# Attention into a token mixer on one core: the hand-ordered steps behind batch 0's first products in another order, with two more filling products

## The chip, the cores and the metric

The kernel runs on one core of one Trainium2 chip. The metric is the device time of one execution in microseconds (us). Three runs of the kernel before gave 104.08, 104.41 and 104.64; the median, 104.41, is what the change is held against.

## The reference

Eight batches, eight heads, 576 tokens, head size 64, float32 in and out. Each batch goes through an attention in two stages over 32 packed queries `p`, and the result goes, heads side by side (576 x 512), into a mixer whose mixing matrix is made from the tokens themselves.

```
p_packed = softmax(p k^T / 8) v            # per head: 32 x 64
x        = softmax(q p_packed^T / 8) p_packed   # per head: 576 x 64, then 576 x 512
wq, wk   = x @ w_q, x @ w_k                # 576 x 64 each
W_tok    = (wq wk^T) / 8                   # 576 x 576, never formed by the kernel
mixed    = W_tok @ x
out      = relu(mixed) @ w_out             # 576 x 512
```

## The kernel before, in words

There is no loop in the program. A string, `ORDER` (lines 13 to 57), lists some 520 steps, and lines 603 to 624 issue them one after the other. Each step runs on one engine, and each engine executes its own steps in the order in which the string has them: a step that has to wait holds back whatever stands behind it on that engine. Semaphores for the data that steps exchange are set by the framework. A token reads `STEP.batch.part@engine=PSUM banks`: `@A` is ScalarE (ACT), `@V` VectorE (DVE), `@P` GpSimd (POOL); matmul steps have no engine and are TensorE's (PE). The eight PSUM banks are named by hand after the `=`.

The steps of one batch b, in the order of their data:

- `LD.kb`, `LD.vb`, `LD.qb` load k, v and q with a cast to bf16. GpSimd issues them, each `LD.v` as two transfers, every other one as one. They share GpSimd's instruction stream with its arithmetic. There are four buffers of each (`NL = 4`).
- `KT` (DVE) transposes k; `S1` (PE) forms the scores of the packed queries; `X1` (ACT) takes the exponential; `TE` (DVE) transposes it; `PV` (PE) multiplies with v and with a column of ones; `RC`, `PP`, `PT` (DVE) divide and transpose. That gives p_packed.
- `QK` (PE) multiplies p_packed with w_k and w_q; `QKE` copies it out of PSUM, and `QD` (POOL) copies a half of it once more.
- `QV` (DVE) transposes q; `S2` (PE) forms the scores of the 576 queries in parts (0 and 1: 256 tokens each, 2: the last 64, 3: 512 tokens); `X2` (ACT) takes the exponential into float32; `RS` and `RR` (DVE) sum and take reciprocals; `AM` multiplies, on POOL or DVE, into bf16; `AT` (PE) transposes and `AE` copies that out.
- `WKQ` (PE) forms wk and wq from it, `WE` copies; `GM`, `GE`, `Y`, `YE` build the small matrix of the mixer; `MX` and `MR` (PE) form the mixed tokens, `RL` and `RLR` apply the relu; `OT.b.0` to `OT.b.3` (PE) multiply 128 tokens each with w_out, `OT.b.4` what remains of two batches (odd b alone); `OE` and `OEF` copy to SBUF, `ST` and `STF` store to memory, nearly all issued by SyncE (SP), a few by POOL.
- `WARM.n=bank` is work without a result: TensorE multiplies zeros, 128n columns in float32, 512 columns at a time unless a second number says otherwise.

Output tiles `o` have six buffers (`NO = 6`, line 8), so batch 6 writes where batch 0 was, and batch 7 where batch 1 was: `OE.6` needs `ST.0` finished. `HOLD.v7` makes SP, whose stores stand behind it, wait until v of batch 7 has landed.

The order of work between `WKQ.0` and `S1.3`, which the prediction walks through, stands on lines 20 to 29. Of GpSimd's steps it holds these, in the kernel before:

```
AM.0.1 LD.q2 LD.O LD.k3 LD.v3 QD.1 AM.1.2 AM.1.0 AM.1.1 LD.k4 QD.2 LD.q3 LD.v4 LD.q4 AM.2.3 AM.2.2 LD.k5
```

Of the kernel before, what the change touches and what calls it, by code (L numbers as in the profile page):

```python
# [28 lines left out]
RL.1.1@A S1.3=2,3,0,1 X1.3.0@A AM.2.2@P OT.1.4=4 TE.3.0@V LD.k5 AT.2.2=5 X1.3.1@A TE.3.1@V AT.2.3=2 AE.2.3@V
LD.v5 MX.1.0=6,7 AE.2.2@V PV.3.0=0,1 PV.3.1 OEF.1.4@A WKQ.2.0=2,3 WKQ.2.1 RC.3@V PP.3.1@V RL.1.0@A WKQ.2.2  # L30
WE.2.2@A OT.1.2=4,5 OT.1.3 PP.3.0@V PT.3@V QK.3=6 OE.1.1@A LD.q5 KT.4.2@V S1.4=0,1,2,3 GM.2=7 OT.1.0=4,5
X1.4.1@A LD.k6 GE.2@A QKE.3@V X1.4.0@A QV.3.2@V TE.4.1@V Y.2=2,3 YE.2@A S2.3.2=6,7 X2.3.2@A S2.3.3=0,1
X2.3.3@A MX.2.0=2,3 TE.4.0@V RL.2.0@A MR.2=6,7 RLR.2@V OT.1.1 MX.2.1=6,7 RL.2.1@A OE.1.0@A PV.4.0=0,1 QD.3@P
PV.4.1 RS.3.4@V RR.3.4@V LD.v6 AM.3.3@P AM.3.2@P RC.4@V OT.2.0=2,3 OT.2.1 LD.q6 OE.2.0@A PP.4.0@V PP.4.1@V
PT.4@V QK.4=6 AT.3.3=7 QV.4.2@V AT.3.2=0 AE.3.2@A LD.k7 S2.4.2=4,5 AE.3.3@V X2.4.2@A S2.4.3=2,3 X2.4.3@A
KT.5.2@V WKQ.3.0=0,1 WKQ.3.1 WKQ.3.2 RS.4.4@V RR.4.4@V QKE.4@A WE.3.2@A S1.5=4,5,2,3 X1.5.1@A LD.v7 TE.5.1@V
OT.2.2=6,7 AM.4.3@P QD.4@P AM.4.2@P GM.3=0 X1.5.0@A TE.5.0@V GE.3@A OT.2.3 Y.3=2,3 YE.3@V PV.5.0=4,5 PV.5.1
HOLD.v7 MR.3=0,1 RC.5@V PP.5.1@V OE.2.1@A MX.3.0=2,3 PP.5.0@V PT.5@V MX.3.1=6,7 RLR.3@A RL.3.0@A OT.3.4=0
RL.3.1@A AT.4.2=1 AE.4.2@A OEF.3.4@A QV.5.2@V AT.4.3=5 AE.4.3@V ST.1.4@P QK.5=4 QKE.5@V QD.5@P S2.5.2=2,3
X2.5.2@A KT.6.2@V S2.5.3=6,7 X2.5.3@A HA.5@P WKQ.4.0=0,1 WKQ.4.2 LD.q7 WKQ.4.1 WE.4.2@A OT.3.0=2,3  # L40
S1.6=4,5,6,7 X1.6.0@A GM.4=0 GE.4@V TE.6.0@V LD.r7 OT.3.1 X1.6.1@A TE.6.1@V Y.4=0,1 OE.3.0@A RS.5.4@V RR.5.4@V
PV.6.0=4,5 YE.4@A PV.6.1 MX.4.0=6,7 RC.6@V RL.4.0@A PP.6.0@V AM.5.3@P PP.6.1@V PT.6@V MX.4.1=2,3 AM.5.2@P
OT.3.2=0,1 OT.3.3 RL.4.1@A QK.6=4 QKE.6@A QV.6.2@V ST.2.1 S2.6.2=6,7 X2.6.2@A S2.6.3=2,3 ST.3.4 MR.4=4,5
# [5 lines left out]
OEF.5.4@A S2.7.1=6,7 ST.5.4 GM.6=3 GE.6@V X2.7.1@A RS.7.1@V RR.7.1@V S2.7.2=0,1 X2.7.2@A S2.7.0=4,5 QK.7=2
X2.7.0@A RS.7.0@V RR.7.0@V Y.6=6,7 YE.6@A OT.5.2=0,1 MX.6.1=4,5 QKE.7@A MX.6.0=6,7 AM.7.1@P RS.7.2@V RR.7.2@V  # L50
MR.6=2,3 OT.5.3 RLR.6@V RL.6.0@V RL.6.1@A OE.5.1@A ST.4.1 AM.7.0@P OT.5.0=2,3 AM.7.2@P AT.7.0=4 AE.7.0@A
AT.7.1=5 AE.7.1@V AT.7.2=6 AE.7.2@V OT.6.2=0,1 OEF.6.2@A QD.7@P WKQ.7.0=4,5 WKQ.7.2 WKQ.7.1 WE.7.0@A WE.7.1@A
STF.6.2 OT.6.0=6,7 OT.6.1 GM.7=0 OE.6.0@V OT.5.1 OE.5.0@V ST.5.1 GE.7@A Y.7=4,5 OT.6.3 OEF.6.3@V ST.6.0
# [599 lines left out]
```

## Time and profile before

| | |
|---|---|
| time, median of three runs | 104.41 us (104.08 to 104.64) |
| span of the profiled execution, first to last instruction | 102.8 us |
| what the median has beyond that span | 1.6 us |
| TensorE busy | 92.7 us, 90% of the span, of which the filling products (line 619) 19.5 |
| VectorE, ScalarE, GpSimd busy | 73.7, 65.0, 51.8 us |
| DMA | 25.13 MB; 84.0% of 16 engines' span in the queue that GpSimd fills |
| granted TensorE clock | 1.000 over the whole span |

The profiled execution comes without a time of its own; its span is set beside the median, and the 1.6 us between them is taken as what lies around the span. In the lines shown below, times are microseconds from the start of the span. "Idle before" an instruction is followed by what ended it ("<-"); a group such as `x8` is eight instructions drawn together. Line numbers (L405) are lines of the kernel; a line can be that of a helper that several steps use. TensorE's steps are told apart by line: L282 is `S1`, L315 `PV`, L336 `QK`, L373 `S2`, L414 and L419 `AT`, L441 and L446 `WKQ`, L467 `GM`, L477 `Y`, L492 `MX`, L498 `MR`, L540 `OT`, L580 the halves of the last `OT`, L619 `WARM`. On GpSimd L405 is `AM`, L173 `LD.v`, L176 `LD.k`, L182 `LD.q`, L166 `LD.O`, L130 `QD`, L561 a whole batch's store.

### The profile page before, as it was taken

What the parts mean: (1) busy time and instruction counts of PE and PEld (TensorE: products, weight loads), DVE (VectorE), ACT (ScalarE), POOL (GpSimd) and SP (SyncE); (2) the same over time, 40 slices, a digit from 0 to 9 for tenths busy, and PEclk for the clock granted to TensorE, in tenths of its full rate; (3) what the DMA queues carried; (4) which work ended last, traced back from release to release, by engine and by line L of the source; (5) the groups of instructions that cost most, each with busy time, mean ns of one, the idle gap of its engine ahead of it and who ended that gap; (6) DMA issues with size and microseconds to landing.
All of it is one profiled execution on the core that took longest, in us unless ns stands there. A gap on an engine that the chain in (4) does not pass through costs nothing.

```text
span 102.8 us, 3593 instructions
## 1 busy us (share of the span) xinstructions
PE 92.7 (90%) x1536; PEld 54.6 (53%) x1536; DVE 73.7 (72%) x140; ACT 65.0 (63%) x111; POOL 51.8 (50%) x81
## 2 busy tenths in 40 slices
PE   5995999998698899999998899989999999999940
...
PEclk9999999999999999999999999999999999999999
DMA  0999999999999999999999999999999999986894
GB/s 9 249 230 207 213 210 213 207 209 213 205 211 207 212 211 210 213 205 212 211 212 207 211 213 204 217 211 203 255 262 409 411 410 408 418 345 264 335 364 160
DMA packets 13279, 25.13 MB, mean 244 GB/s; under 512 B 1040, under 2 KB 6416, under 8 KB 13008
## 3 DMA queue, kind: packets, MB, share of 16 engines
q0 software_dynamic: 9648, 17.04, 84.0%
...
q8 instruction: 12, 0.20, 0.7%
...
## 4 chain that ended last, share of the span: by engine, by line
PE 49%; DMA 21%; DVE 8%; POOL 7%; ACT 6%; issue 3%; SPq 1%; DVEq 0%; POOLq 0%; ACTq 0%
PE ps L540 26%; DMA q_sb<-in_q_dram 13%; DMA o<-in_moe_w_q_dram 8%; PE ps L373 4%; POOL a L405 4%; PE ps L315 3%; ACT e1T L293 3%; PE ps L419 3%; PE ps L446 3%; DVE rs L394 2%; PE ps L441 2%; PE ps L467 2%; PE ps L282 2%; ACT e L378 1%; DVE qT L237 1%
## 5 line engine op out<-in xcount | busy, mean ns | idle before, releaser
L540 PE MATMUL ps<-wout,relu 128*128 128x512 bf16 x124 | 30.6, 380 | 0.0
L405 POOL TENSOR_TENSOR a<-e,rr 128x256 bf16<-128x256 f32 (+2 forms) x18 | 19.5, 1099 | 17.9 <-DVE rr L399 7.0
L619 PE MATMUL ps<-o 128*128 128x128 f32 (+3 forms) x76 | 19.5, 401 | 1.2 <-DVE o L135 1.2
L540 PEld LDWEIGHTS <-relu 128*128 128x128 bf16 x124 | 10.7, 98 | 11.7 <-issue 1.1
L128 ACT ACTIVATE o<-ps 128x1024 f32<-128x1024 f32 (+2 forms) x13 | 11.3, 871 | 5.4 <-PE ps L540 5.2
L619 PEld LDWEIGHTS ps<-o 128*128 128x128 f32 x76 | 11.3, 209 | 5.2 <-issue 3.6
L503 ACT ACTIVATE relu<-ps 128x1024 bf16<-128x1024 f32 (+1 forms) x14 | 13.0, 968 | 1.1 <-PE ps L492 1.1
L293 ACT ACTIVATE e1T<-ps 128x576 bf16<-128x576 f32 x16 | 9.8, 656 | 5.8 <-PE ps L282 5.2
L378 ACT ACTIVATE e<-ps 128x256 f32<-128x256 f32 (+2 forms) x19 | 11.2, 623 | 2.7 <-PE ps L373 2.5
L394 DVE TENSOR_REDUCE rs<-e 128x16 f32<-128x512 f32 (+2 forms) x13 | 10.9, 840 | 2.3 <-ACT e L378 2.2
L237 DVE STREAM_TRANSPOSE kT<-k_sb 128x1152 uint32<-128x1152 uint32 (+1 forms) x9 | 11.1, 1230 | 1.9 <-DMA k_sb<-in_k_dram 1.9
L173 POOL DMA_DIRECT2D v_sb<-in_v_dram x16 | 10.0, 628 | 4.0 <-DMA v_sb<-in_v_dram 1.6
L237 DVE STREAM_TRANSPOSE qT<-q_sb 128x1152 uint32<-128x1152 uint32 (+1 forms) x10 | 11.0, 1108 | 0.1
L132 DVE COPY o<-ps 128x1024 f32<-128x1024 f32 (+2 forms) x7 | 6.8, 977 | 5.3 <-PE ps L540 2.7
L237 DVE STREAM_TRANSPOSE e<-e1T 128x288 uint32<-128x288 uint32 x16 | 7.4, 468 | 3.1 <-ACT e1T L293 2.7
L128 ACT ACTIVATE aT<-ps 128x128 bf16<-128x128 f32 (+2 forms) x11 | 5.0, 465 | 5.7 <-PE ps L419 3.3
L128 ACT ACTIVATE wkq<-ps 128x448 bf16<-128x448 f32 (+1 forms) x10 | 7.2, 730 | 1.8 <-PE ps L446 1.7
L315 PE MATMUL ps<-v_sb,e 64*64 64x192 bf16 x288 | 7.5, 245 | 0.8 <-DVE e L237 0.5
L315 PEld LDWEIGHTS <-e 64*64 64x64 bf16 x288 | 5.9, 107 | 2.6 <-DVE e L237 2.1
L373 PEld LDWEIGHTS <-qT 64*128 64x128 bf16 x320 | 5.4, 94 | 2.8 <-DVE qT L237 1.7
L373 PE MATMUL ps<-ppT,qT 64*128 64x64 bf16 x320 | 6.6, 190 | 0.2 <-DVE qT L237 0.2
L446 PE MATMUL ps<-aT,pqk 128*128 128x256 bf16 (+1 forms) x48 | 6.8, 246 | 0.0
...
## 6 DMA issues: line engine op xcount, KB each, us to landing
v_sb<-in_v_dram POOLq DMA_DIRECT2D x16, 288.0 KB, 13.9
...
k_sb<-in_k_dram POOLq DMA_DIRECT2D x7, 576.0 KB, 13.6
q_sb<-in_q_dram POOLq DMA_DIRECT2D x6, 576.0 KB, 13.6
out_dram<-o POOLq DMA_DIRECT2D x2, 1024.0 KB, 11.3
...
q_sb<-in_q_dram POOLq DMA_DIRECT2D x4, 288.0 KB, 10.4
...
```

What stands on the lines that cost most here:

```text
L128: nc.scalar.activation(o, i, COPY)
L173: nc.gpsimd.dma_start(v_bufs[b % NL][halves(i), 0:7:2], src)
L237: nc.vector.transpose(o, i)
L293: nc.scalar.activation(e1T[:, x], T["s1", b][x].rearrange("a c m -> a m c"), EXP, scale=scale)
L315: nc.tensor.matmul(T["pv", b][halves(cc), i], lhsT, rhs, start=n == 0, stop=n == R - 1, skip_group_check=True)
L373: nc.tensor.matmul(ps[:, y, t - t0, i], lhsT, rhs, start=e == 0, stop=e == 1)
L378: nc.scalar.activation(e2[:, t0:t1].rearrange("a t (i y n) -> a y (t i) n", i=2, y=2), T["s2", b, c].rearrange("a y t i n -> a y (t i) n") ...
L394: nc.vector.tensor_reduce(rs[:, t0 * H:t1 * H], src, axis=AX, op=ADD)
L405: e.tensor_tensor(a2[:, t0:t1].rearrange("a t i (u l) -> a (t i u) l", l=L), e2v(b, c), T["rr", b][:, t0 * H:t1 * H].to_broadcast((P, (t1 ...
L503: nc.scalar.activation(o, i, RELU)
L540: nc.tensor.matmul(ps, lhsT, wout[:, j, :], start=j == 0, stop=j == NJ - 1)
L619: nc.tensor.matmul(bank(int(bk), [w]), warm[:, 0:P], rhs, start=True, stop=True)
```

## The change

Only the string is changed. Up to `WARM.6=6` behind `PT.0`, nothing differs; from `QK.0` to `AT.0.1` only PSUM banks differ. From there on, the same steps stand in another order, 36 of them on another engine (31 between ScalarE and VectorE in either direction, five `AM` between GpSimd and VectorE), many on other PSUM banks, and two more `WARM.3` stand among TensorE's steps. No step of the computation is added or taken away. Behind `AM.0.1`, GpSimd's steps read

```
LD.q2 LD.O LD.k3 LD.v3 LD.k4 LD.q3 QD.1 LD.v4 AM.1.0 AM.1.1 LD.q4 LD.k5 QD.2 AM.2.3 AM.2.2 LD.v5
```

with `AM.1.2` now on VectorE. The first `-` and `+` lines of the diff, and those of its end that hold batch 0's and 1's stores (`ST.0.8`, `ST.1.8`):

```diff
-X1.0.0@A TE.0.0@V WARM.8=4 PV.0.0=4,5 PV.0.1 RC.0@V PP.0.0@V PP.0.1@V LD.q1 PT.0@V WARM.6=6 QK.0=6 QKE.0@A
-QV.0.0@V QV.0.1@V QD.0@P WARM.4=7 S2.0.2=2,3 X2.0.2@A RS.0.2@V RR.0.2@V S2.0.0=0,1 LD.v2 S2.0.1=4,5 X2.0.0@A
-RS.0.0@V RR.0.0@V X2.0.1@A RS.0.1@V RR.0.1@V AM.0.2@P WARM.6=7 AT.0.2=7 AE.0.2@A AM.0.0@P WARM.5=6 AT.0.0=6
-KT.1.2@V AM.0.1@P WARM.3=2 AT.0.1=7 AE.0.1@A AE.0.0@V WKQ.0.0=2,3 WKQ.0.2 WE.0.0@A LD.q2 WKQ.0.1 KT.2.2@V
-S1.1=0,1,4,5 WE.0.1@A GM.0=6 X1.1.0@A TE.1.0@V GE.0@A WARM.2=7 Y.0=2,3 YE.0@V S1.2=0,1,6,7 MR.0=2,3 X1.1.1@A
-TE.1.1@V MX.0.0=4,5 X1.2.0@A LD.O PV.1.0=0,1 TE.2.0@V PV.1.1 X1.2.1@A TE.2.1@V RC.1@V LD.k3 PP.1.0@V PP.1.1@V
-PT.1@V MX.0.1=6,7 QV.1.2@V RLR.0@A QK.1=2 QKE.1@V RL.0.0@A WARM.3=3 S2.1.2=4,5 S2.1.0=0,1 RL.0.1@A X2.1.2@A
-RS.1.2@V RR.1.2@V S2.1.1=2,3 X2.1.0@A RS.1.0@V RR.1.0@V WARM.1=6 PV.2.0=6,7 PV.2.1 X2.1.1@A RS.1.1@V RC.2@V
-LD.v3 QD.1@P AM.1.2@P AT.1.2=4 RR.1.1@V AM.1.0@P WARM.5=5 AT.1.0=5 AM.1.1@P LD.k4 PP.2.0@V AE.1.2@A PP.2.1@V
-PT.2@V QK.2=4 AE.1.0@A QKE.2@A QD.2@P QV.2.2@V LD.q3 LD.v4 AT.1.1=0 AE.1.1@A WKQ.1.0=2,3 WKQ.1.2 WKQ.1.1
-WE.1.0@V S2.2.2=6,7 WE.1.1@A X2.2.2@A S2.2.3=4,5 X2.2.3@A GM.1=1 OT.0.0=2,3 GE.1@V Y.1=6,7 OT.0.1 YE.1@A
-RS.2.4@V OE.0.0@A MR.1=0,1 MX.1.1=4,5 RLR.1@A RR.2.4@V OT.0.2=6,7 LD.q4 OT.0.3 KT.3.2@V AM.2.3@P OE.0.1@V
...
-OE.4.0@A ST.0.8@P WKQ.5.1 RS.6.4@V WE.5.2@A RR.6.4@V ST.3.0 ST.4.0 ST.1.8@P S1.7=2,3,6,7 X1.7.1@A AM.6.3@V
...
+WARM.8=4 PV.0.0=4,5 PV.0.1 RC.0@V PP.0.0@V PP.0.1@V LD.q1 PT.0@V WARM.6=6 QK.0=0 QKE.0@A QV.0.0@V QV.0.1@V QD.0@P
...
+RS.0.1@V RR.0.1@V AM.0.2@P WARM.6=1 AT.0.2=0 AE.0.2@A AM.0.0@P WARM.5=1 AT.0.0=0 KT.1.2@V AM.0.1@P WARM.3=1
+AT.0.1=1 AE.0.1@A AE.0.0@V WKQ.0.0=6,7 WKQ.0.2 WE.0.0@A LD.q2 WKQ.0.1 WARM.1=2 WE.0.1@A LD.O S1.1=2,3,4,5 X1.1.0@A
+LD.k3 KT.2.2@V TE.1.0@V X1.1.1@A WARM.2=0 WARM.3=0 GM.0=0 TE.1.1@V PV.1.0=6,7 PV.1.1 RC.1@V GE.0@V S1.2=2,3,4,5
+PP.1.0@V PP.1.1@V PT.1@V WARM.3=1 QV.1.2@V X1.2.0@A QK.1=0 Y.0=6,7 LD.v3 YE.0@V QKE.1@A X1.2.1@A TE.2.1@V LD.k4
+LD.q3 WARM.3=1 S2.1.2=2,3 S2.1.0=0,1 X2.1.2@A S2.1.1=4,5 TE.2.0@V RS.1.2@V X2.1.0@A RS.1.0@V QD.1@P LD.v4
+MX.0.0=6,7 MX.0.1=2,3 RR.1.2@V RR.1.0@V X2.1.1@A PV.2.0=0,1 PV.2.1 WARM.5=4 AM.1.2@V RL.0.0@A RS.1.1@V RC.2@V
+PP.2.0@V RR.1.1@V AM.1.0@P RL.0.1@A AT.1.0=4 PP.2.1@V AT.1.2=5 AE.1.2@A PT.2@V AM.1.1@P AE.1.0@A WKQ.1.2=6,7 QK.2=0
+AT.1.1=1 LD.q4 QV.2.2@V WKQ.1.0 MR.0=2,3 LD.k5 RLR.0@A AE.1.1@V S2.2.3=4,5 S2.2.2=2,3 X2.2.3@A QKE.2@V QD.2@P
+WKQ.1.1 X2.2.2@A RS.2.4@V WE.1.1@A RR.2.4@V OT.0.2=0,1 WE.1.0@A AM.2.3@P OT.0.3 GM.1=2 GE.1@V OT.0.0=4,5 Y.1=6,7
...
+OT.5.0=4,5 AE.7.1@V AE.7.0@A ST.0.8@P QKE.7@A MX.6.0=6,7 MX.6.1=0,1 QD.7@P MR.6=2,3 RL.6.0@A RLR.6@V RL.6.1@A
+OT.5.1 WKQ.7.1=2,3 WKQ.7.2 ST.1.8@P WKQ.7.0 OT.6.0=6,7 WE.7.1@V WE.7.0@A GM.7=0 OT.6.1 OE.5.0@A ST.5.1 ST.5.0
...
```

More of the change, by code (lines that the diff above doesn't have):

```diff
@@ L13 @@
 ORDER = """
-LD.N0@A LD.N1@S SET.warm@V SET.v0@V SET.aT0@V SET.aT1@V SET.aT2@V SET.idf@V LD.W0@A LD.W1@S SET.tab@A LD.h0
-LD.g0 LD.v0 LD.r0 LD.q0 LD.k1 NC.0@V PX.0@V NC.1@A PX.1@V SET.aff@P SET.idb@V SET.v3@P KT.0.0@V SET.mask@P
-WC.1@P WC.0@P LD.k2 SET.v1@P LD.v1 SET.v2@P KT.0.1@V WARM.4=0 WARM.22.128=0 S1.0=0,1,2,3 X1.0.1@A TE.0.1@V
-X1.0.0@A TE.0.0@V WARM.8=4 PV.0.0=4,5 PV.0.1 RC.0@V PP.0.0@V PP.0.1@V LD.q1 PT.0@V WARM.6=6 QK.0=6 QKE.0@A
-QV.0.0@V QV.0.1@V QD.0@P WARM.4=7 S2.0.2=2,3 X2.0.2@A RS.0.2@V RR.0.2@V S2.0.0=0,1 LD.v2 S2.0.1=4,5 X2.0.0@A
@@ L29 @@
[L29 to L43, printed above, removed]
@@ L44 @@
-X2.6.3@A OE.3.1@V RLR.4@V KT.7.2@V AT.5.2=6 AE.5.2@A AT.5.3=7 OT.4.0=0,1 OT.4.1 AE.5.3@A WKQ.5.0=4,5 WKQ.5.2
-OE.4.0@A ST.0.8@P WKQ.5.1 RS.6.4@V WE.5.2@A RR.6.4@V ST.3.0 ST.4.0 ST.1.8@P S1.7=2,3,6,7 X1.7.1@A AM.6.3@V
-OT.4.2=0,1 GM.5=4 TE.7.1@V OT.4.3 AT.6.3=5 X1.7.0@A TE.7.0@V GE.5@A OE.4.1@A AM.6.2@P AT.6.2=4 ST.2.0 Y.5=6,7
-YE.5@A ST.3.1 PV.7.0=2,3 QV.7.1@V AE.6.3@V QV.7.0@V AE.6.2@A QD.6@P PV.7.1 RC.7@V PP.7.0@V PP.7.1@V PT.7@V
-MR.5=0,1 RLR.5@A MX.5.1=6,7 RL.5.1@A MX.5.0=4,5 RL.5.0@V WKQ.6.0=0,1 WKQ.6.1 WKQ.6.2 WE.6.2@A OT.5.4=2
@@ L49 @@
[L49 to L53, printed above, removed]
@@ L54 @@
-STF.6.3 YE.7@A ST.5.0 MR.7=6,7 RLR.7@A MX.7.0=4,5 RLF.7.0.1@A RLF.7.0.0@V MX.7.1=2,3 RLF.7.1.0@A OT.7.4=0
-OEF.7.4@A ST.7.4 RLF.7.1.1@V OT.7.1=6 OEF.7.1@V OT.7.0=7 STF.7.1 OT.7.2=1 OEF.7.0@A OH.7.0=0 STF.7.0 OEF.7.2@A
-STF.7.2 OEH.7.0@V STH.7.0 OH.7.1=5 OEH.7.1@A STH.7.1@A
+LD.N0@A LD.N1@S SET.warm@V SET.v0@V SET.aT0@V SET.aT1@V SET.aT2@V SET.idf@V LD.W0@A LD.W1@S SET.tab@A LD.h0 LD.g0
+LD.v0 LD.r0 LD.q0 LD.k1 NC.0@V PX.0@V NC.1@A PX.1@V SET.aff@P SET.idb@V SET.v3@P KT.0.0@V SET.mask@P WC.1@P WC.0@P
@@ new lines @@
+LD.k2 SET.v1@P LD.v1 SET.v2@P KT.0.1@V WARM.4=0 WARM.22.128=0 S1.0=0,1,2,3 X1.0.1@A TE.0.1@V X1.0.0@A TE.0.0@V
+WARM.8=4 PV.0.0=4,5 PV.0.1 RC.0@V PP.0.0@V PP.0.1@V LD.q1 PT.0@V WARM.6=6 QK.0=0 QKE.0@A QV.0.0@V QV.0.1@V QD.0@P
+WARM.4=6 S2.0.2=6,7 X2.0.2@A RS.0.2@V RR.0.2@V S2.0.0=2,3 LD.v2 S2.0.1=4,5 X2.0.0@A RS.0.0@V RR.0.0@V X2.0.1@A
+RS.0.1@V RR.0.1@V AM.0.2@P WARM.6=1 AT.0.2=0 AE.0.2@A AM.0.0@P WARM.5=1 AT.0.0=0 KT.1.2@V AM.0.1@P WARM.3=1
+AT.0.1=1 AE.0.1@A AE.0.0@V WKQ.0.0=6,7 WKQ.0.2 WE.0.0@A LD.q2 WKQ.0.1 WARM.1=2 WE.0.1@A LD.O S1.1=2,3,4,5 X1.1.0@A
@@ new lines @@
+AT.1.1=1 LD.q4 QV.2.2@V WKQ.1.0 MR.0=2,3 LD.k5 RLR.0@A AE.1.1@V S2.2.3=4,5 S2.2.2=2,3 X2.2.3@A QKE.2@V QD.2@P
+WKQ.1.1 X2.2.2@A RS.2.4@V WE.1.1@A RR.2.4@V OT.0.2=0,1 WE.1.0@A AM.2.3@P OT.0.3 GM.1=2 GE.1@V OT.0.0=4,5 Y.1=6,7
+OE.0.1@A YE.1@A OT.0.1 KT.3.2@V AM.2.2@P OE.0.0@V S1.3=0,1,2,3 AT.2.3=6 AE.2.3@V AT.2.2=7 AE.2.2@V MX.1.0=4,5
+X1.3.1@A X1.3.0@A MX.1.1=2,3 WKQ.2.0=0,1 MR.1=6,7 RL.1.0@A TE.3.1@V TE.3.0@V LD.v5 WKQ.2.1 RL.1.1@A PV.3.0=4,5
+PV.3.1 RLR.1@A WKQ.2.2 RC.3@V WE.2.2@A PP.3.0@V KT.4.2@V PP.3.1@V OT.1.2=2,3 OT.1.3 S1.4=6,7,0,1 GM.2=4 OT.1.4=5
@@ new lines @@
+PT.3@V QV.3.2@V OE.1.1@A GE.2@A X1.4.1@A QK.3=4 Y.2=2,3 X1.4.0@A S2.3.2=0,1 QKE.3@V OEF.1.4@V YE.2@A X2.3.2@A
+S2.3.3=6,7 LD.q5 X2.3.3@A MR.2=2,3 OT.1.0=0,1 QD.3@P MX.2.1=4,5 MX.2.0=6,7 TE.4.0@V TE.4.1@V RS.3.4@V RLR.2@A
+RR.3.4@V RL.2.0@A PV.4.0=2,3 LD.k6 PV.4.1 RC.4@V RL.2.1@A OT.1.1 AM.3.2@V LD.q6 PP.4.0@V OT.2.0=6,7 PP.4.1@V
+QV.4.2@V AT.3.2=2 OT.2.1 PT.4@V LD.v6 AM.3.3@P OE.1.0@A OE.2.0@A AT.3.3=3 S2.4.3=4,5 S2.4.2=0,1 AE.3.2@V
+WKQ.3.2=6,7 X2.4.3@A AE.3.3@V WKQ.3.0 WKQ.3.1 X2.4.2@A KT.5.2@V RS.4.4@V OT.2.2=2,3 S1.5=4,5,0,1 WE.3.2@A QK.4=6
@@ new lines @@
+RR.4.4@V X1.5.0@A X1.5.1@A GM.3=7 OT.2.3 TE.5.0@V GE.3@A TE.5.1@V Y.3=4,5 YE.3@V AM.4.2@P QKE.4@V OE.2.1@A
+PV.5.0=0,1 PV.5.1 MR.3=4,5 MX.3.1=6,7 MX.3.0=2,3 RLR.3@A RC.5@V PP.5.1@V PP.5.0@V AT.4.2=4 OT.3.4=5 RL.3.1@A PT.5@V
+AM.4.3@P QD.4@P LD.k7 LD.v7 QV.5.2@V RL.3.0@A AT.4.3=0 QK.5=1 AE.4.2@A S2.5.2=6,7 S2.5.3=2,3 QKE.5@A AE.4.3@V
+WKQ.4.1=0,1 WKQ.4.0 WKQ.4.2 OEF.3.4@V X2.5.2@A OT.3.0=6,7 KT.6.2@V X2.5.3@A HA.5@P LD.q7 S1.6=4,5,2,3 WE.4.2@A
+GM.4=0 LD.r7 X1.6.1@A OT.3.1 GE.4@A Y.4=2,3 X1.6.0@A RS.5.4@V YE.4@A OT.3.2=0,1 RR.5.4@V MX.4.0=4,5 OE.3.0@A
@@ new lines @@
+MX.4.1=2,3 TE.6.0@V RL.4.0@A AM.5.2@V OT.3.3 AM.5.3@P TE.6.1@V RL.4.1@A AT.5.2=6 QD.5@P PV.6.0=4,5 PV.6.1 ST.1.4@P
+QV.6.2@V AE.5.2@A AT.5.3=2 RC.6@V PP.6.1@V PP.6.0@V OE.3.1@A OT.4.2=6,7 PT.6@V KT.7.2@V AE.5.3@A S2.6.2=4,5
+S2.6.3=0,1 WKQ.5.2=2,3 X2.6.2@A WKQ.5.0 X2.6.3@A RS.6.4@V WKQ.5.1 HOLD.v7 WE.5.2@A OT.4.3 S1.7=4,5,0,1 X1.7.0@A
+OT.4.0=2,3 RR.6.4@V X1.7.1@A ST.3.4 GM.5=4 OT.4.1 TE.7.0@V TE.7.1@V PV.7.0=0,1 AM.6.2@V QV.7.1@V PV.7.1 GE.5@V
+OE.4.1@A QK.6=5 Y.5=6,7 AM.6.3@P OE.4.0@A AT.6.3=4 MR.4=2,3 YE.5@A RC.7@V PP.7.0@V PP.7.1@V QKE.6@A MR.5=6,7
```

8 lines of the change are left out of this document (added).

## The prediction, written before the changed kernel ran

> **What bounds the kernel now.** I read the page's slices first, then the chain of waits in order of time, then busy time in two stretches.
>
> ```profile
> PE   5995999998698899999998899989999999999940
> PEclk9999999999999999999999999999999999999999
> DMA  0999999999999999999999999999999999986894
> ```
>
> TensorE and the DMA engines are both busy to nine tenths nearly throughout, and the clock was granted in full. Which of the two sets the end is told by the chain:
>
> ```profile
> 13.89 13.59 DMA q_sb<-in_q_dram
> 27.51 1.39 DVE qT L237
> 28.94 0.31 PE ps L373 x8
> ```
>
> Up to 27.48 us (13.89 + 13.59) the chain is the load of q of batch 1. It is transposed, and at 28.94 TensorE begins `S2.1`. From there the chain is almost all TensorE:
>
> ```profile
> 28.94:35.68 6.74, 6.14 (x156) 4.48 (x157) 5.14 (x13) 3.71 (x9) 5.25 (x9) 1.00 1.16 210
> 35.68:98.97 63.29, 61.68 (x1044) 34.49 (x1038) 50.35 (x85) 49.48 (x81) 28.41 (x36) 1.00 1.08 271
> ```
>
> The columns are the stretch, its length, then busy time of PE, PEld, DVE, ACT, POOL. TensorE is idle for 0.60 us (6.74 - 6.14) up to the end of `S2.2` and for 1.61 us (63.29 - 61.68) from there to its last product. So no order can win much more than 2.2 us behind 28.94, and the start at 28.94 belongs to the load of q1, whose place among the loads does not change. Any time that TensorE newly loses behind 28.94 is paid almost in full.
>
> **The change ahead of S2.1.** Two idle places and the filler that is doubled:
>
> ```profile
> 27.51 0.41 PE L336 MATMUL ps<-wqk,ppT 64*64 64x128 bf16 x8 [0.97 <-DVE ppT L237]
> 27.85 0.91 PE L619 MATMUL ps<-o 128*128 128x384 f32 x2
> ```
>
> A `WARM.3` is 0.91 us; two more are 1.8 us. They stand ahead of `S2.1`, where TensorE waits for q1 in any case (0.97 us ahead of `QK.1` alone), and they take the place of `MX.0` and `MR.0`, which move behind `S2.1`. What moves costs later:
>
> ```profile
> 24.60 0.23 PE L498 MATMUL ps<-wkq,y 64*128 64x64 bf16 x4
> ...
> 85.14 0.61 PE L492 MATMUL ps<-wkq,y 64*128 64x512 bf16 x4
> ```
>
> `MX` with four products is 0.61 with its drain, 0.5 to the next step, and `MR` 0.2: 0.7 us of real work that now lies behind 28.94. The idle 0.97 and these 0.7 make room for 1.7 of the fillers' 1.8 us, so I cost the fillers at nothing; with that cover gone, `S2.1` would start up to 1.8 us late.
>
> **From S2.1 to S2.2: GpSimd's queue.** This is the term that decides. GpSimd issues the loads itself, between its multiplications `AM`. Its timeline shows that an issue can hold the engine:
>
> ```profile
> 12.15 1.24 POOL L173 DMA_DIRECT2D v_sb<-in_v_dram  x2 [0.30 <-POOL v_sb L206]
> ...
> 16.25 1.24 POOL L173 DMA_DIRECT2D v_sb<-in_v_dram  x2 [0.20 <-POOL pqk L130]
> ...
> 20.66 0.76 POOL L182 DMA_DIRECT2D q_sb<-in_q_dram  x1
> ...
> 24.36 0.61 POOL L173 DMA_DIRECT2D v_sb<-in_v_dram  x1 [0.82 <-DMA v_sb<-in_v_dram]
> ...
> 31.34 2.05 POOL L405 TENSOR_TENSOR a<-e,rr 128x512 bf16<-128x512 f32 x2 [0.22 <-DVE rr L399]
> ...
> 34.31 0.70 POOL L182 DMA_DIRECT2D q_sb<-in_q_dram  x1
> ...
> 46.60 0.71 POOL L176 DMA_DIRECT2D k_sb<-in_k_dram  x1 [2.09 <-DMA q_sb<-in_q_dram]
> ```
>
> and the DMA issues, asked for around those times (last column: us to landing), say when these landed, in the order v1, v2, q2, q3:
>
> ```profile
> v_sb<-in_v_dram POOLq DMA_DIRECT2D x2, 288.0 KB, 10.9
> v_sb<-in_v_dram POOLq DMA_DIRECT2D x2, 288.0 KB, 12.5
> q_sb<-in_q_dram POOLq DMA_DIRECT2D x1, 576.0 KB, 11.9
> q_sb<-in_q_dram POOLq DMA_DIRECT2D x1, 576.0 KB, 12.0
> ```
>
> k of batch 6 was issued at 46.60, 2.09 us late, when q3 (34.31 + 12.0 = 46.3) had landed. k6 goes to a buffer that has nothing to do with q3; but q3 is the eighth transfer ahead of it in GpSimd's list (q3, two of v4, q4, k5, two of v5, q5). Likewise the second half of v3 waited until 24.36 for a half of v1 (12.77 + 10.9 = 23.7, by the median of the two), again the eighth ahead. So GpSimd has at most eight loads on their way, and the ninth holds the engine until the oldest has landed.
>
> In the kernel before, no load stands between `LD.v3` and `AM.1.1`; `LD.k4` follows. In the changed order `LD.k4`, `LD.q3` and both halves of `LD.v4` stand in front of `AM.1.0` and `AM.1.1`. Counting back eight: k4 waits for q1 (27.48), q3 and the first half of v4 for the halves of v2 (16.25 + 12.5 = 28.8 and, 0.6 later, 29.4), the second half of v4 for q2: 20.66 + 11.9 = 32.56. Its issue takes 0.62, so `AM.1.0` starts at 33.2 and, at 1.02 each, ends at 34.25; `AM.1.1` ends at 35.3. In the kernel before the pair ended at 33.39.
>
> TensorE gets there earlier:
>
> ```profile
> 30.07 0.94 PE L315 MATMUL ps<-v_sb,e 64*64 64x192 bf16 x36
> ...
> 31.24 1.32 PE L619 MATMUL ps<-o 128*128 128x512 f32 x4
> ...
> 33.45 0.40 PE L419 MATMUL ps<-idb,a 128*128 128x128 bf16 x4 [0.18 <-POOL a L405]
> ...
> 34.97 0.78 PE L373 MATMUL ps<-ppT,qT 64*128 64x64 bf16 x40
> 35.68 0.47 PE L467 MATMUL ps<-wkq,a 128*128 128x64 bf16 x10
> ```
>
> 28.94 + `S2.1` 0.71 (as `S2.2`, 34.97 to 35.68) + `MX.0` 0.5 + `PV.2` 0.9 + `WARM.5` 1.2 = 32.25. There it waits until 34.3, about 2 us. In the kernel before, `AT.1.1`, `WKQ.1` and `S2.2` take from 33.45 to 35.68, 2.23 us. The changed order has behind 34.3 the same, plus `AT.1.0` (0.2), `QK.2` (0.4) and `MR.0` (0.2): it ends at 37.35. All steps that the kernel before had done at 35.68 are then done here too. **First term: 37.35 - 35.68 = +1.7 us.**
>
> Its bounds: if GpSimd's wait did not exist, VectorE would be the gate, since two `TE.2` and `YE.0` now run behind the transposed q1, ahead of `RS.1`:
>
> ```profile
> L237 DVE STREAM_TRANSPOSE e<-e1T 128x288 uint32<-128x288 uint32 x16 | 7.4, 468 | 3.1 <-ACT e1T L293 2.7
> L486 DVE TENSOR_SCALAR y<-ps 128x256 bf16<-128x256 f32 x2 | 0.8, 425 | 0.3 <-PE ps L477 0.3
> ```
>
> that is 2 x 0.47 + 0.43 = 1.4 us, of which 0.8 was idle or other work before: +0.6. With neither wait, TensorE's own sum ends 0.7 earlier than before. Above, +2.2, if `AE.1.2` adds its time between `AT.1.2` and `WKQ.1.2`. I take the value from GpSimd's rows.
>
> **From S2.2 to the end.** The same steps, so the same 61.68 us of TensorE; what can differ is the idle 1.61. The largest two stalls of the kernel before are
>
> ```profile
> 54.90 0.62 PE L419 MATMUL ps<-idb,a 128*128 128x128 bf16 x8 [0.44 <-POOL a L405]
> ...
> 68.58 0.94 PE L315 MATMUL ps<-v_sb,e 64*64 64x192 bf16 x36 [0.47 <-DVE e L237]
> ```
>
> and with another order these can go. New ones come, for example right behind `S2.2`: both `WE.1` now stand on ScalarE behind `X2.2` (before, one ran on VectorE ahead of it).
>
> ```profile
> 35.08 0.54 ACT L128 ACTIVATE wkq<-ps 128x448 bf16<-128x448 f32 x1 [0.60 <-PE ps L446]
> 35.52 1.35 ACT L378 ACTIVATE e<-ps 128x256 f32<-128x256 f32 x2
> ...
> 38.47 1.90 PE L540 MATMUL ps<-wout,relu 128*128 128x512 bf16 x8
> ```
>
> 1.35 + 2 x 0.54 = 2.4 us against `WKQ.1.1` 0.3 and two `OT` 1.9 on TensorE: `GM.1` waits 0.2 to 0.3. I find like places, of 0.1 to 0.4 each, where `OE.0.0` stands on VectorE ahead of `AE.2` and the `TE.3` that `PV.3` needs, where `S2.3.3` needs the banks that the second `X1.4` empties, and where `OT.2.0` needs `RL.2.1`. They are about ten; taken at 0.2, 2.2 us with the first, where 1.61 was. **Second term: +0.6**, bounded by -1.6 (no idle left) and +1.6 (twice as much).
>
> **The sum.** TensorE ends at 98.97 + 1.7 + 0.6 = 101.3; the last copies and stores behind it have the same shape, 3.83 us. Span 105.1; with the 1.6 us that the median has beyond the span, 106.7 us, 2.2% above 104.41. About 0.5% is what a measurement can tell from no change here.
>
> **Rivals.** *The late stores hold ScalarE (slower still).* `ST.0.8` moves behind `AM.7.0` on GpSimd, and `OE.6.0` must wait for it, as it overwrites the same buffer.
>
> ```profile
> 72.28 1.29 POOL L561 DMA_DIRECT2D out_dram<-o  x2
> ...
> 84.96 2.63 POOL L405 TENSOR_TENSOR a<-e,rr 128x512 bf16<-128x512 f32 x3 [6.36 <-ACT y L484]
> ```
> ```profile
> out_dram<-o POOLq DMA_DIRECT2D x2, 1024.0 KB, 11.3
> ```
>
> `AM.7` ended at 87.6; about a microsecond later the store is issued, and 11.3 later it would land at about 100, when `OE.6.0` is due near 94. Those 11.3 us were shared with the last loads. It decides if landing takes over 5 us. The Trainium skill, "DMA: Bandwidth & Descriptors", section "Anatomy of one DMA", gives 2.0 us plus the bytes over 436 GB/s, an estimate of 4.4 us, by which nothing would wait; no run here shows so large a store alone. Halfway, 2.5 us more: 109.2. Chance 0.20.
>
> *The clock falls.* TensorE's longest idle place so far behind the first products is 0.97 us, at a granted clock of 1.00; 2 us are not shown. If 3.1 us of products behind it ran at half speed: 109.8. The Trainium skill, "TensorE: Matmul & The Clock Gate", section "Why this matters for your kernels", allows idle gaps up to about 3 us, so by it nothing would fall. Chance 0.04.
>
> *The terms cancel.* The wait is there, but the rest loses its 1.61 us of idle: 104.41 + 1.7 - 1.6 = 104.5. Chance 0.09.
>
> *The order pays (faster).* GpSimd does not hold `AM.1.0`, VectorE's extra work hides, and TensorE's own sum counts: -0.7, and half the later idle gone, -0.8: 102.9. For it: the later stalls are few and short, and such an order may avoid them. Against it: the row at 46.60. It decides if `AM.1.0` starts by 31.4. Chance 0.12.
>
> **How the numbers follow.** The forecast has 0.55, at 106.7. Its own bounds (first term +0.6 to +2.2, second -1.6 to +1.6, seldom at their ends together) give 105.0 to 108.2; the store rival carries the range to 109.2. From 104.9 to 109.2 leaves out the faster case, part of the cancelling one, and the worst of the stores. Faster 0.12, same 0.09, slower 0.79.
>
> **What would show it.** Right: GpSimd's issue of a half of v4 that ends its wait at about 32.6 for q of batch 2, `AM.1.0` near 33.2, an idle place of 1.5 to 2 us on TensorE ahead of the first transposes near 34.3, `S2.2` ending near 37, TensorE idle for about 2 us behind it, its last product near 101.3. Wrong: `AM.1.0` before 32, the order paying; or `OE.6.0` waiting for a store, the tail costing more than the head.

## The result, and the profile after

| | before | changed |
|---|---|---|
| median time | 104.40 us (104.08 to 104.64) | 111.70 us (110.90 to 112.44) |
| ratio, 95% interval | | 1.0704 (1.0642 to 1.0767) |
| profiled execution: span | 102.8 us | 109.0 us (time 110.90) |
| `S2.1` starts | 28.94 | 28.93 |
| all steps up to `S2.2` and `WKQ.1` done | 35.68 | 38.53 |
| TensorE's last product ends | 98.97 | 103.94 |
| from there to the end | 3.83 | 5.06 |

The change costs 7.3 us, more than three times the 2.3 that were forecast. The direction and the first cause were right; the size was not, and 111.7 lies outside the range of 104.9 to 109.2. A second measurement of the changed kernel, beside the last experiments, gave 111.80 us and 1.0695 (1.0662 to 1.0727). Every ratio is taken to the kernel before as it ran beside the kernel in question, and leaves out an execution that is over 1.5% above the fastest of its kernel (one each of y3 and z1 below), which the medians include.

The span grew by 6.2 us, and the table divides it: 2.85 up to 38.53, 2.12 from there to TensorE's last product, 1.23 behind it. This execution took 110.90 us; it is the fastest of the four, 0.8 below their median. In the changed kernel and the runs built on it, line numbers are one lower than in the kernel before (`AM` is L404). The page of the changed kernel, its slices for TensorE, the granted clock and DMA:

```profile
PE   5999999989781999899999999997996999999910
PEclk9999999999999759999999999999999999999999
DMA  1999999999999999999999999999950948999892
```

Three marks were not in the page before: a hole in TensorE (7, 8, 1) around slice 13, a fall of the clock (7, 5) right behind it, and holes in DMA (5, 0, 4) at slices 30 to 33. Busy time by stretch, with the columns as before (PE first; the granted clock, the DMA share and GB/s last):

```profile
28.93:38.53 9.60, 6.87 (x163) 5.07 (x163) 6.18 (x17) 5.01 (x9) 4.74 (x8) 0.92 1.16 209
38.53:103.94 65.41, 62.02 (x1022) 34.60 (x1037) 50.00 (x87) 51.69 (x83) 26.88 (x33) 0.99 0.99 250
37.00:38.00 1.00, 1.00 (x42) 0.91 (x35) 0.29 (x1) 0.52 (x2) 0.00 (x0) 0.50 1.20 205
79.00:84.00 5.00, 4.17 (x96) 2.22 (x95) 4.90 (x8) 3.78 (x5) 1.91 (x1) 1.00 0.33 132
103.94:109.00 5.06, 0.00 (x1) 0.00 (x0) 0.37 (x1) 0.28 (x1) 0.00 (x0) 0.97 0.60 218
```

TensorE is idle for 2.73 us in the first stretch (0.60 before) and for 3.39 in the second (1.61 before). The clock was granted at a half around 37 us. The chain of waits, in order of time, shows what ends the first hole:

```profile
20.35 12.08 DMA q_sb<-in_q_dram
...
32.97 0.10 POOL v_sb L172
...
33.59 1.07 POOL a L404
...
34.71 0.40 PE ps L418 x4
```

and the timelines of GpSimd and TensorE the same place:

```profile
27.75 0.71 POOL L175 DMA_DIRECT2D k_sb<-in_k_dram  x1 [3.23 <-DMA q_sb<-in_q_dram]
...
32.96 0.61 POOL L172 DMA_DIRECT2D v_sb<-in_v_dram  x1 [1.92 <-DVE pp L322]
```
```profile
34.71 0.40 PE L418 MATMUL ps<-idb,a 128*128 128x128 bf16 x4 [2.31 <-POOL a L404]
```

k of batch 4 waited 3.23 us for q of batch 1, and the second half of v of batch 4 was issued at 32.96, when q of batch 2 had landed (20.35 + 12.08 = 32.43). The row names a VectorE step as the one that ended this wait; the chain names the load. Behind it `AM.1.0` starts at 33.59, and TensorE has been idle for 2.31 us.

### The profile page after: what moved, and what is told of

The parts are those of the page before. It is cut to its first block, busy times and chain, and to the rows that moved or that the text cites. A ratio compares the mean times of both kernels' runs of the same rounds, so it can differ in the third digit from the quotient of the medians.

```text
span 109.0 us, 3573 instructions
## 1 busy us (share of the span) xinstructions
PE 95.2 (87%) x1523; PEld 56.8 (52%) x1540; DVE 73.7 (68%) x144; ACT 66.7 (61%) x110; POOL 50.9 (47%) x78
## 4 chain that ended last, share of the span: by engine, by line
PE 54%; DVE 16%; DMA 11%; ACT 8%; issue 3%; POOL 3%; DVEq 0%; POOLq 0%; ACTq 0%
PE ps L539 17%; PE ps L618 12%; DMA q_sb<-in_q_dram 11%; PE ps L372 4%; DVE rs L393 4%; PE ps L314 3%; PE ps L418 3%; ACT relu L502 3%; POOL a L404 3%; PE ps L445 2%; DVE kT L236 2%; ACT e1T L292 2%; PE ps L440 2%; PE ps L491 2%; PE ps L281 2%
## 5 line engine op out<-in xcount | busy, mean ns | idle before, releaser
L539 PE MATMUL ps<-wout,relu 128*128 128x512 bf16 x110 | 29.6, 387 | 0.9 <-issue 0.4
L404 POOL TENSOR_TENSOR a<-e,rr 128x512 bf16<-128x512 f32 (+2 forms) x15 | 18.2, 1232 | 17.9 <-DVE rr L398 17.3
L618 PE MATMUL ps<-o 128*128 128x128 f32 (+3 forms) x80 | 21.8, 420 | 1.2 <-DVE o L134 1.2
L127 ACT ACTIVATE o<-ps 128x1024 f32<-128x1024 f32 (+2 forms) x16 | 14.4, 900 | 6.3 <-PE ps L539 5.3
L618 PEld LDWEIGHTS ps<-o 128*128 128x128 f32 x80 | 12.8, 222 | 5.8 <-issue 4.0
L502 ACT ACTIVATE relu<-ps 128x1024 bf16<-128x1024 f32 (+1 forms) x16 | 14.3, 947 | 1.3 <-PE ps L491 0.9
L127 ACT ACTIVATE aT<-ps 128x128 bf16<-128x128 f32 (+2 forms) x10 | 4.4, 450 | 6.3 <-PE ps L413 3.5
L418 PE MATMUL ps<-idb,a 128*128 128x128 bf16 x64 | 5.5, 220 | 2.6 <-POOL a L404 2.3
L175 POOL DMA_DIRECT2D k_sb<-in_k_dram x7 | 5.1, 726 | 5.4 <-DMA q_sb<-in_q_dram 3.2
L445 PE MATMUL ps<-aT,pqk 128*128 128x256 bf16 (+1 forms) x48 | 7.5, 252 | 0.0
```

What stands on the lines that cost most here:

```text
L127: nc.scalar.activation(o, i, COPY)
L404: e.tensor_tensor(a2[:, t0:t1].rearrange("a t i (u l) -> a (t i u) l", l=L), e2v(b, c), T["rr", b][:, t0 * H:t1 * H].to_broadcast((P, (t1 ...
L502: nc.scalar.activation(o, i, RELU)
L539: nc.tensor.matmul(ps, lhsT, wout[:, j, :], start=j == 0, stop=j == NJ - 1)
L618: nc.tensor.matmul(bank(int(bk), [w]), warm[:, 0:P], rhs, start=True, stop=True)
```

## The experiments

Three marks, three theories: GpSimd's list holds `AM.1` (and the clock falls behind the hole); the late stores leave DMA idle and lengthen the tail; the steps on VectorE and ScalarE are slower in the new order. Each was undone in the changed order or put alone into the order before.

| kernel | median us | ratio to before, 95% interval |
|---|---|---|
| changed, loads behind `AM.1.1` (x1) | 108.45 | 1.0401 (1.0385 to 1.0418) |
| changed, the hole filled (x2) | 110.36 | 1.0599 (1.0560 to 1.0637) |
| changed, stores early (x3) | 110.26 | 1.0566 (1.0543 to 1.0589) |
| before, loads in front (x4) | 107.79 | 1.0333 (1.0311 to 1.0355) |
| changed, loads and stores (y1) | 106.97 | 1.0242 (1.0203 to 1.0281) |
| the same, and `AM` on GpSimd (y2) | 105.23 | 1.0067 (1.0024 to 1.0110) |
| changed, without two fillers (y3) | 111.23 | 1.0640 (1.0592 to 1.0688) |
| before, stores late (y4) | 107.17 | 1.0266 (1.0223 to 1.0308) |
| changed, `AM` on GpSimd alone (z1) | 109.84 | 1.0482 (1.0429 to 1.0535) |
| before, `AM.6.3` on GpSimd (z2) | 104.80 | 1.0030 (1.0011 to 1.0050) |
| y2 and three more places (z3) | 105.10 | 1.0055 (1.0036 to 1.0074) |

**x1, the loads behind `AM.1.1`.** GpSimd's list:

```diff
 LD.v3
-LD.k4
-LD.q3
 QD.1@P
-LD.v4
 AM.1.0@P
 AM.1.1@P
+LD.k4
+LD.q3
+LD.v4
 LD.q4
```

> The changed order, with the loads of k4, q3 and v4 moved behind AM.1.1 in GpSimd's list, where the kernel before has them. Theory A (GpSimd held by its ninth load, 2.3 us of TensorE idle, and the clock that falls to a half behind it): AM.1.0 starts near 31.4 instead of 33.6, the idle place ahead of AT.1 shrinks below 0.7 us, granted clock 1.00 throughout, time 106.5 to 108 instead of about 111.5. Theory B (the new order of arithmetic steps is what costs, and the hold only shows where the time is lost first): above 110.

Its timelines of GpSimd and TensorE, and the stretch behind TensorE's last product:

```profile
31.50 1.04 POOL L404 TENSOR_TENSOR a<-e,rr 128x512 bf16<-128x512 f32 x1 [3.31 <-DVE rr L398]
```
```profile
32.60 0.40 PE L418 MATMUL ps<-idb,a 128*128 128x128 bf16 x4
```
```profile
101.25:106.80 5.55, 0.00 (x0) 0.00 (x0) 0.37 (x1) 0.28 (x1) 0.00 (x0) 0.69 0.49 176
```

`AM.1.0` starts 2.1 us earlier, and the first transposes follow the fillers without a wait. The time falls by 3.3 us (1.0704 - 1.0401 of 104.4, 3.2, by the first measurement of the changed kernel; 3.1 by the second), to 108.45, 0.45 above what theory A expected. The tail of 5.55 us is 0.5 longer than that of the changed kernel.

**x4, the same four transfers in front, in the order before.** `LD.k4` and `LD.q3` ahead of `QD.1`, `LD.v4` ahead of `AM.1.0`; nothing else.

> The kernel before with one thing of the change: the loads of k4, q3 and v4 moved ahead of AM.1.0 and AM.1.1. Theory A: AM.1.0 starts near 33.2 instead of 31.3, TensorE idle near 2 us ahead of AT.1.0; without a fall of the clock 106 to 106.7, with it up to 109. Theory B: within 0.7 us of the kernel before.

```profile
33.25 0.61 POOL L173 DMA_DIRECT2D v_sb<-in_v_dram  x1 [1.82 <-DMA q_sb<-in_q_dram]
```
```profile
34.99 0.61 PE L419 MATMUL ps<-idb,a 128*128 128x128 bf16 x4 [2.73 <-POOL a L405]
```
```profile
36.00:40.00 4.00, 3.95 (x77) 2.81 (x74) 0.92 (x2) 2.94 (x6) 1.00 (x2) 0.72 1.19 209
```

Here the row itself names q of batch 2. The place in the list alone makes the hole, behind which the clock falls (0.72 between 36 and 40 us), and costs 3.5 us. Theory A holds from both sides.

**x2, the hole filled.** How much of that is the wait and how much the clock?

```diff
-WARM.5=4
+WARM.16=4
```

> The changed order, with WARM.16 instead of WARM.5 ahead of AT.1.0, so that filling products cover the idle 2.3 us; the wait for GpSimd stays. If the fall of the clock has a cost of its own: granted clock 1.00, 1.5 to 3 us faster than the changed kernel, 108.5 to 110. If the wait alone counts: within 0.5 us of it, whatever the clock.

```profile
30.66 3.70 PE L618 MATMUL ps<-o 128*128 128x512 f32 x8
34.58 0.40 PE L418 MATMUL ps<-idb,a 128*128 128x128 bf16 x4 [0.21 <-POOL a L404]
```
```profile
36.00:40.00 4.00, 3.95 (x80) 2.64 (x80) 1.98 (x3) 2.71 (x6) 1.22 (x3) 1.00 1.18 208
```

The first transposes start as late as in the changed kernel (34.58 against 34.71), but the clock stays at 1.00, and the time is 1.0 us less (1.0695 - 1.0599) than the second measurement of the changed kernel, 1.1 less than the first. So the fall of the clock costs about 1 us, less than expected, and the wait itself about 2 of x1's 3.2. The 1 us is a mean: the clock was at a half for 3.4 us in the changed kernel's profile above (36.98 to 40.4), and for about 7 us in that of its second measurement (111.73 us).

**y3, without the two added fillers.** The two `WARM.3` ahead of and behind `QK.1` and `Y.0` taken out.

> The changed order without the two WARM.3 between S1.2 and S2.1. As costed, they lie where TensorE waits for q of batch 1: S2.1 still starts near 28.9 and the time stays within 0.5 us of the changed kernel (111 to 112). Were they on the path: 1.5 us faster. Were they what keeps the clock up ahead of the wait for GpSimd: slower by 0.5 to 2 us at a lower granted clock.

```profile
26.96 0.30 PE L335 MATMUL ps<-wqk,ppT 64*64 64x128 bf16 x4 [0.94 <-DVE ppT L236]
...
28.27 0.78 PE L372 MATMUL ps<-ppT,qT 64*128 64x64 bf16 x40 [0.85 <-DVE qT L236]
```
```profile
28.00:32.00 4.00, 3.73 (x81) 2.73 (x82) 3.87 (x13) 3.53 (x6) 1.65 (x3) 0.64 1.16 212
```

The time is the changed kernel's (intervals overlap), so the fillers cost nothing there, as forecast. But without them there are two idle places of 0.94 and 0.85 us whose ends lie 1.3 us apart, and behind them the clock falls to a mean of 0.64 between 28 and 32 us, where it was 1.00 in the changed kernel. (It is not so each time: one of y3's four executions, of 110.60 us, has a mean clock of 1.000.) This fall does not show in the time, since `AM.1.0` is late in any case.

**x3, the stores of batches 0 and 1 early.** In GpSimd's list:

```diff
 ST.1.4@P
+ST.0.8@P
+ST.1.8@P
...
 AM.7.0@P
-ST.0.8@P
 QD.7@P
-ST.1.8@P
```

> The changed order, with the stores of batches 0 and 1 (ST.0.8, ST.1.8) right behind ST.1.4 in GpSimd's list, as early as in the kernel before. If the DMA engines' idle stretch near 80 to 84 us and the stores pushed behind it lengthen the tail: the stretch from TensorE's last product to the end falls from 5.1 to 3.8 us, time 1.0 to 1.5 us less than the changed kernel. If not: within 0.5 us of it.

```profile
79.00:84.00 5.00, 4.89 (x108) 2.88 (x108) 4.17 (x6) 4.59 (x6) 1.91 (x1) 1.00 1.01 422
...
104.99:108.90 3.91, 0.00 (x1) 0.00 (x0) 0.37 (x1) 0.28 (x1) 0.00 (x0) 0.79 0.60 217
```

DMA, which stood at a share of 0.33 between 79 and 84 us, is full there, the tail is 3.91 us again, and the time falls by 1.4 us, by the medians. (The execution shown lost more at the half clock than the one of the changed kernel, so that its last product ends later, at 104.99.) **y1** puts x1 and x3 together:

> The changed order with both list places of GpSimd undone: the loads of k4, q3, v4 behind AM.1.1, and the stores ST.0.8, ST.1.8 right behind ST.1.4. If the two costs are separate and add up: 1.5 to 1.9 us below the kernel with the loads alone moved (108.45), 106.5 to 107.0, the tail behind TensorE's last product 3.8 to 4.0 us instead of 5.6. If the loads' move already took the stores' cost: above 108.

The tail is 3.86 us and the time 1.5 us below x1 (1.7 by the ratios): the two costs are separate and add up.

**y4, late stores in the order before.** `ST.0.8` behind `AM.7.2`, `ST.1.8` behind `QD.7`.

> The kernel before with one thing of the change: ST.0.8 and ST.1.8 as late in GpSimd's list as in the changed order, behind AM.7 and QD.7. If late stores lengthen the tail: TensorE's last product near 99 as before, the tail 5 to 5.6 us instead of 3.8, time 105.3 to 106.2. If the tail has another cause: within 0.4 us of the kernel before.

Its timelines of ScalarE and TensorE:

```profile
91.86 0.60 ACT L128 ACTIVATE o<-ps 128x512 f32<-128x512 f32 x1 [3.48 <-DMA out_dram<-o]
```
```profile
92.94 0.28 PE L467 MATMUL ps<-wkq,a 128*128 128x64 bf16 x4 [1.54 <-ACT wkq L128]
```

It costs 2.9 us, 1 us more than expected. The tail is 4.62 us (100.88 to 105.50), 0.8 longer than before; the other 1.9 are lost ahead of TensorE's last product, by another way: `OEF.6.2` stands early on ScalarE here, has to wait 3.48 us until batch 0's store has left its buffer, and holds `WE.7` and so TensorE. This is the rival that the prediction had named, in the order before; in the changed order the first `OE.6` comes later, and the price is paid in the tail.

**y2, `AM.5.2` and `AM.6.2` back on GpSimd.** The reason first. In the changed kernel, VectorE's `AM` of one size, and what GpSimd did meanwhile:

```profile
31.06 0.36 DVE L404 TENSOR_TENSOR a<-e,rr 128x256 bf16<-128x256 f32 x1
...
72.14 2.10 DVE L404 TENSOR_TENSOR a<-e,rr 128x256 bf16<-128x256 f32 x1
...
81.73 1.46 DVE L404 TENSOR_TENSOR a<-e,rr 128x256 bf16<-128x256 f32 x1
```
```profile
72.06 1.91 POOL L404 TENSOR_TENSOR a<-e,rr 128x1024 bf16<-128x1024 f32 x1 [0.37 <-DVE rr L398]
...
81.01 1.91 POOL L404 TENSOR_TENSOR a<-e,rr 128x1024 bf16<-128x1024 f32 x1 [6.06 <-DVE rr L398]
```

The work of 0.36 us takes 2.10 and 1.46 when GpSimd has begun an `AM` of its own: each ends about 0.25 us behind GpSimd's. Behind the second stand `QV.7` and `GE.5` on VectorE, and TensorE waits:

```profile
84.12 0.25 PE L476 MATMUL ps<-pp,g 64*64 64x128 bf16 x4 [0.90 <-DVE g L131]
```

The edit on top of y1 (where `AM.6.2` had stood on VectorE ahead of `QV.7.1`):

```diff
-AM.5.2@V
+AM.5.2@P
 AM.5.3@P
...
-AM.6.2@V
 AM.6.3@P
+AM.6.2@P
```

> As the kernel with loads and stores moved, and AM.5.2 and AM.6.2 on GpSimd again (AM.5.2 ahead of AM.5.3, AM.6.2 behind AM.6.3) instead of VectorE. In the changed kernel these two took 2.10 and 1.46 us on VectorE while GpSimd ran an AM, where the same work alone took 0.36. If that collision holds up VectorE's chain: 0.6 to 1.5 us faster than without this edit, idle places ahead of AT.5.2 and Y.5 gone. If VectorE has room for it: within 0.3 us.

1.7 us less than y1 (106.97 to 105.23), where 1.5 was the most expected. Both pairs of `AM` now take 2.48 us on GpSimd, and what is left of `AM` on VectorE runs in 0.36 and 0.43:

```profile
68.97 2.48 POOL L404 TENSOR_TENSOR a<-e,rr 128x256 bf16<-128x256 f32 x2 [0.38 <-DVE rr L398]
```
```profile
28.70:99.03 70.33, 67.48 (x1183) 38.89 (x1200) 52.66 (x102) 56.55 (x91) 33.32 (x42) 1.00 1.08 264
```

TensorE needs 70.33 us from `S2.1` to its last product, of which it is idle for 2.85 by these records; the kernel before needs 70.03. **z1** does this edit alone in the changed order:

> The changed order with AM.5.2 and AM.6.2 on GpSimd again, and nothing else: the loads still hold AM.1, the stores are still late. If the collision of the two engines' AM has its own cost on the way to the end: 1.2 to 1.8 us less than the changed kernel run beside it. If that time only shortens a wait that the late stores at the end then take back: within 0.5 us.

> The changed kernel itself, on the chip of its neighbours here, as the yardstick for the kernel with AM on GpSimd alone: 111 to 112 us if the time does not depend on the chip.

109.84 against 111.80: 2.0 us (by the ratios 2.2), a little above the 1.2 to 1.8 expected, with the other two faults in place. Its profiled execution (108.91 us) is the fastest of its four and shows one thing more. The hole ahead of `AT.1.0` is there, longer than in the changed kernel's profile, but the clock does not fall behind it:

```profile
34.84 0.40 PE L418 MATMUL ps<-idb,a 128*128 128x128 bf16 x4 [2.81 <-POOL a L404]
```
```profile
PEclk9999999999999999999999999999999999999997
```

In its other executions the mean clock is 0.956 to 0.972, and they still take 109.52 to 110.93 us, against 111.52 to 111.89 for the changed kernel beside them. So x1, x3 and z1 take 3.2, 1.4 and 2.2 us alone, 6.8 in all, and 6.6 together (1.0704 to 1.0067).

**z2 and z3, for a kernel that beats both.** Before has one such meeting too: `AM.6.3` on VectorE beside `AM.6.2` on GpSimd, which took 1.58 us. z2 moves `AM.6.3` to GpSimd. z3 takes on what y2 leaves: `YE.0` and `GE.1` on ScalarE, `MX.0.0` ahead of `S2.1`.

> The kernel before, with AM.6.3 on GpSimd instead of VectorE. There the two engines meet as well: AM.6.3 (1.23 us on VectorE) and AM.6.2, which takes 1.58 us on GpSimd where its like takes 0.6. If VectorE, full from 72 to 80 us, holds TensorE there: 0.2 to 0.6 us faster than before. If TensorE's own work is what counts there: within 0.2 us.

> As the kernel with loads, stores and AM repaired (105.23), and what is left in TensorE's idle places taken on: YE.0 on ScalarE, so that VectorE's chain behind q of batch 1 is 0.4 us shorter and MX.0.0 fits ahead of S2.1, and GE.1 on ScalarE, so that Y.1 does not wait for RS.2 and RR.2. If these places are what is left of the new order's cost: 0.4 to 0.8 us faster, 104.4 to 104.8, no worse than the kernel before. If the rest is somewhere else: 105 or more.

Neither pays: z2 is 0.3% slower than before, outside both of its cases, and z3 0.55%, as y2, which is its case "somewhere else". Of z3's idle places the largest has moved and grown:

```profile
41.24 0.62 PE L418 MATMUL ps<-idb,a 128*128 128x128 bf16 x8 [0.70 <-POOL a L404]
```

`Y.1` no longer waits, but `AT.2.3`, next in line, waits for `AM.2.3`, 0.70 us instead of 0.31 in y2. No version that was run beats the kernel before.

## Why the prediction was wrong

**Right.** What bounds the kernel, the start of `S2.1` (28.93 against 28.94; that it agrees to 0.01 is chance, as in the other profiled executions of the new order it lies between 28.27 and 29.14), the fillers at nothing, and the step that was to decide: the eight transfers in flight, the second half of v4 that waits for q2, `AM.1.0` late (33.59 against 33.2), TensorE waiting ahead of `AT.1.0` (2.31 us against 2.0).

The stretches of the sum, in us, in the traces of six orders. z4 is the changed kernel's second measurement; z1 and y2 have `AM.5.2` and `AM.6.2` on GpSimd, and y1 and y2 have the loads behind `AM.1.1` and the stores early:

| stretch | before | changed | z4 | x2, hole filled | z1, `AM` | y1, loads and stores | y2, all three |
|---|---|---|---|---|---|---|---|
| `S2.1` starts, to `S2.2` and `WKQ.1` done | 6.74 | 9.60 | 11.53 | 9.42 | 9.79 | 6.91 | 6.91 |
| from there to the last product | 63.29 | 65.41 | 65.04 | 65.55 | 63.71 | 65.49 | 63.42 |
| behind it | 3.83 | 5.06 | 5.12 | 5.13 | 5.12 | 3.86 | 3.87 |

**The first term was mis-sized: +1.7 was forecast, 2.85 measured.** The stretch was to end at 37.35 and ended at 38.53. About 0.4 of these 1.2 us is the issue of v4's second half, which begins 0.53 us behind q2's landing (32.43 to 32.96) instead of at once. About 0.3 is the wait for `AE.1.2` (0.37 us in the changed kernel, in x2 and in y2), which the prediction named as a bound and left out of its value: from the first transposes on, x2 needs 3.34 us at a clock of 1.00, where 3.05 were forecast. The remaining 0.5 is the clock (3.82 us against x2's 3.34), which the prediction had as a rival with a chance of 0.04, on the ground that an idle place of 2 us was not yet shown. The half clock came, though its price is around 1 us (x2) and not the 3.1 of the rival. In the changed kernel's second profile (z4), with the longer half clock, the stretch ends at 39.84, 4.16 us later than before. The Trainium skill, "TensorE: Matmul & The Clock Gate", section "Why this matters for your kernels", allows idle gaps up to about 3 us. The measurement decides: 2.31 us were enough in the changed kernel's profile, and in y3's two places of less than 1 us close together; in z1's, 2.81 us were not. The length of an idle place alone does not settle it here, and what does stays open.

**The second term was mis-sized: +0.6 was forecast, 2.12 measured.** The step that failed is the move of `AM.5.2` and `AM.6.2`, which was costed at nothing, with no row looked at for it. By the table's second row, the kernels that keep the two on VectorE need 65.0 to 65.6 us, whatever the clock did before; with the two on GpSimd it is 63.4 to 63.7, and 63.29 in the kernel before. So the meeting of the two engines costs 1.8 to 2.1 us (x2 to z1, y1 to y2), and the order of all the rest 0.1 to 0.4, where about ten small waits had been put at +0.6. Of these waits some were there (`MX.1.0` waited 0.29 us for `OE.0.0`). A row that priced the move stood in the profile before: GpSimd's `AM.6.2`, of the size that takes 0.61 there, took 1.58 while VectorE ran `AM.6.3`.

```profile
76.79 1.58 POOL L405 TENSOR_TENSOR a<-e,rr 128x256 bf16<-128x256 f32 x1 [3.22 <-DVE rr L399]
```
```profile
76.67 1.23 DVE L405 TENSOR_TENSOR a<-e,rr 128x1024 bf16<-128x1024 f32 x1
```

The Trainium skill says why in "SBUF — State Buffer", section "Who interferes with whom": a VectorE instruction with both inputs in SBUF and a GpSimd instruction that reads SBUF need one port, and whichever starts first keeps it to its end. The traces agree in both directions: at 76.67 VectorE was first and GpSimd ended 0.47 us behind it; at 72.06 GpSimd was first.

**The tail was costed at no change; it grew by 1.23 us.** The step that failed is "the same shape". The late stores were a rival, but by way of `OE.6.0`, which in the changed order never waited for them: it began at 96.94, and batch 0's store had landed at 95.95, 4.8 us after its issue at 91.15. That is near the 4.4 that the prediction had worked out from the Trainium skill's formula; batch 1's store, issued at 93.19 when other stores were under way, took 6.7.

```profile
out_dram<-o POOLq DMA_DIRECT2D x1, 1024.0 KB, 4.8
```

The bytes were what counted. DMA had nothing to move around 82 us, and two megabytes came back at the end. The prediction never set these bytes against DMA's free time, though the slices before show DMA full there.

By the medians the change cost 5.0 us more than forecast (111.7 against 106.7). The two `AM` account for about 1.9, the tail for 1.2, the clock for 1.0, the issue and `AE.1.2` for 0.7; these are 4.8 together.

Whether the order would pay without these faults can be judged from y2: with the three repaired it is still 0.7% (0.2 to 1.1) slower than before. In its profiled execution, the fastest of six (104.71 us), the stretch from `S2.1` to the last product is only 0.3 us longer than before. Where the rest lies is open; z3's three places were not it, or were paid back next door.
